# First blocks scored against their own 64 keys, and four steps of the opening list moved, in a fused attention and expert kernel

## The chip, the cores and the metric

The kernel runs on one core of a Trainium2 chip. The metric is the device time of one execution in microseconds (us); lower is better. Instruction names below are those of the profile: PE is TensorE (PEld its weight loads), DVE is VectorE, ACT is ScalarE, POOL is GpSimd and SP is SyncE.

## The reference

Two stages follow one another. The first is causal attention with a sliding window of 64 positions, for 8 batches, 8 heads, 576 positions and 64 values a head. The second takes the 4608 rows of 512 values through two weight matrices with a gate between them.

```python
scores = scale * np.matmul(q, k.transpose(0, 1, 3, 2))       # scale = 1/8
rel = pos[:, None] - pos[None, :]
mask = (rel >= 0) & (rel < 64)
scores = np.where(mask, scores, -1000000000.0)
attn = softmax(scores);  attn_out = attn @ v                 # (8, 8, 576, 64)
x = attn_out.transpose(0, 2, 1, 3).reshape(4608, 512)
h = x @ w_in                                                 # 512 -> 2048
out = (h * np.cos(h)) @ w_out                                # 2048 -> 512
```

## The kernel before, in words

**Attention.** The 576 positions of a head are cut into 9 blocks of 64. A *unit* (b, p, j) is block j of a pair p of heads in batch b: 128 rows (two heads) of queries. A block sees its own 64 keys and the 64 before them, so the scores of a unit are a tile of 128 rows and 128 columns. Block 0 has no keys before it; it is given the 128 keys from position 0, and the mask (line 323, `mask[:, 0]`, whose second half is the constant `NEG`) removes the second 64. There are 32 such first blocks, 4 in each batch.

Units are worked in groups of up to four (`groups`). A group n passes through these functions, whose names in the opening list stand in brackets: `g_scores` (s, Gs) lets PE write the scores into a PSUM bank; `g_max` (m, Gm) adds the mask on DVE and takes the row's extreme, into a tile `s`; `g_exp` (e, Ge) takes the exponential on ACT with its row sum `den`, into a tile `e` (6 buffers); `g_inv` (i, Gi) takes the reciprocal of the sums on DVE; `g_norm` (n, Gn) multiplies, on POOL or DVE, into a tile `w`; `g_trans` (w, Gw, Gc) transposes `w` on PE or by a DMA of SP; `values` (v, V) multiplies with v on PE. Groups 0 to 7 (`n < n_first`, batch 0) get their mask from an extra matmul into PSUM instead, and their exponentials read PSUM directly.

For b = 0 and 1 the two heads of a pair are scored by two matmuls of 64 rows each (L309), which run side by side in two halves of the array; transposes of q and k for these batches (tq, tk, Tq, Tk; L216) are of the same kind. From b = 2 on, one matmul with 128 rows does both heads (L303).

**The second stage** works in 9 tiles of 512 tokens. `first` and `first_half` (h; L448, L412) make h, ACT its sine (S; L590, L418), DVE the product (g; L593, L424), and `second_part` (o; L431) and L604 the output. Attention for the batch ahead is worked between the matmuls of a tile.

**Order.** Each engine runs its instructions in the order in which they are recorded. From tile 1 on, a plan with due times (`at`, `pump`) sets it. The start and tile 0 follow a list written out by hand, `FIRST` (lines 50 to 72), of steps such as `Tk.3` (transpose k of batch 1, pair 3), `Pk.3.d` (copy it out on DVE), `Gs.16.4` (scores of group 16 into bank 4), `o.1.0` (second quarter of output block 0: four matmuls), `Lwi.2` (third load of w_in, issued from POOL's queue), `n.1.0.p` (normalise the first group of pair 1 on POOL) and `yB.p` (copy a piece of batch 1's v to the other half of the partitions on POOL). Groups 9 to 16 are batch 1: 9, 11, 13, 15 hold blocks 0 to 3 of the four pairs, 10, 12, 14, 16 blocks 4 to 6; 8 is the last block of batch 0, and 17 and 18 are blocks 7 and 8 of batch 1.

Of the kernel before, what the change touches and what calls it, by code (L numbers as in the profile page):

```python
# [10 lines left out]
def _safe_warn(msg, *a, **kw):  # L11
# [5 lines left out]
AF = mybir.ActivationFunctionType  # L17
# [34 lines left out]
    "Lq0.2 tq.1 tk.1 m.0.0 pq.1.a ms.3.d s.0.1.1 Lk0.2 tq.2 pk.1.d s.1.0.2 Lq0.3 Lk0.3 tk.2 s.1.1.3 "  # L52
    "e.0.0 tq.3 m.0.1 Lq1.0 Lk1.0 Lq1.1 pq.2.d pk.2.d Lk1.1 tk.3 m.1.0 s.2.0.4 Lv0.0 Lv0.1 Tq.0 Lv0.2 "
    "pk.3.d m.2.0 e.0.1 pq.3.a i.0.0 e.1.0 Tk.0 s.3.0.0 Tq.1 e.2.0 Lv0.3 Lwi.0 Pq.0.d i.1.0 Lwi.1 m.3.0 "
    "m.1.1 i.2.0 Pk.0.a e.3.0 Lwi.2 Tk.1 n.1.0.p s.2.1.1 Pq.1.d Gs.10.2 m.2.1 Gs.9.4 n.0.0.p Pk.1.a "
    "n.2.0.p i.3.0 e.1.1 w.0.0 zA.0.d w.1.0 c.0.0.d Gs.12.0 w.2.0 n.3.0.p i.0.1 c.1.0.d zA.1.d c.2.0.d "
    "e.2.1 zB.0.s zB.1.s n.0.1.p i.1.1 w.3.0 v.0.0 c.3.0.d x.0.0.a s.3.1.3 Gm.10 v.1.0 m.3.1 i.2.1 "
    "Gs.11.2 Gm.9 Gm.12 n.1.1.p x.1.0.a e.3.1 ms.4.d w.0.1 w.1.1 c.1.1.a i.3.1 h.0.0.1 h.0.1.4 tb "
# [2 lines left out]
    "g.0.3 S.0.4 ms.6.d h.0.6.0 h.1.1.3 S.0.5 S.1.0 Lq1.2 S.0.6 g.0.4 S.1.1 g.1.0 h.1.2.2 Lk1.2 ms.7.d "  # L61
    "Lq1.3 h.0.7.4 g.0.5 h.1.3.1 Lv1.0 Lwo.1 g.1.1 S.1.2 h.1.4.3 g.0.6 Lk1.3 S.0.7 h.1.5.0 g.1.2 h.1.6.2 "
    "Lwo.2 g.0.7 S.1.3 S.1.4 S.1.5 Lwo.3 h.1.7.4 Lv1.1 S.1.6 g.1.3 g.1.4 S.1.7 g.1.5 Lv1.2 g.1.6 tb2 "
    "Tk.2 Lv1.3 Pk.2.d Ge.10 Tq.2 Pq.2.d Tq.3 Ge.9 Ge.12 o.0.0.1 Pq.3.d Tk.3 o.1.0 Pk.3.d Lv0.4 Lq2.0 "
    "Ge.11 Gs.14.3 Gi.10 Gm.14 g.1.7 Lq2.1 Gs.13.0 Lq2.2 o.0.1.2 Gi.9 o.2.0 Ge.14 Gn.10.p Gm.13 Gc.10 "
    "Gi.12 Gs.8.3 o.1.1 Gs.16.4 Gm.8 o.3.0 Ge.13 o.2.1 Gs.15.0 Gi.11 oc.0.d Gn.9.p o.3.1 Gn.12.p o.0.2.3 "
    "Gi.14 Gm.15 Gs.17.1 oc.1.d Gc.9 Gn.11.p Gi.13 Gm.16 o.1.2 Ge.8 Ge.16 Ge.15 y.1.d Gn.14.p yA.p Gi.8 "
    "Gc.12 Gm.17 o.0.3.0 Gi.16 Gn.13.p yB.p Gc.11 Gn.8.p Lq2.3 Lq2.4 Lq2.5 o.2.2 Gn.16.d Gw.8 Gc.14 "
    "Gc.13 Lk2.0 Gp.8.d o.3.2 Gi.15 Gw.16 Lk2.1 Ge.17 Lk2.2 o.1.3 Gn.15.d V.0 Gp.16.d oc.2.a Gw.15 Gi.17 "
    "Lk2.3 o.2.3 V.1 Gp.15.d X.0.a Gn.17.d X.1.d V.2 V.3 X.2.a X.3.d Gc.17 o.3.3 oc.3.a Gs.18.4 Gm.18 "  # L70
    "Ge.18 Lk2.4 Gi.18 Gn.18.d Gc.18 Lk2.5 Lv1.4 "
# [4 lines left out]
def kernel(  # L76
# [9 lines left out]
    nc = tc.nc  # L86
    B, H, S, D = q.shape
    assert (B, H, S, D) == (8, 8, 576, 64)
    scale = 1.0 / math.sqrt(D)
# [28 lines left out]
    mask = const.tile([128, 3, 128], F32, name="mask")  # L118
# [14 lines left out]
    def bank(which, name):  # L133
        return ps.tile([128, 512], F32, tag=which, name=name)
# [133 lines left out]
    groups = [[(0, p, j) for j in range(GF * g, GF * g + GF)] for p in range(PAIRS) for g in range(TU // GF)]  # L268
    n_first = len(groups)
# [12 lines left out]
    def g_scores(n, which):  # L282
        s_ps = bank((BANKS if n < n_listed else S_BANKS)[which], "s_ps")
        units = groups[n]
        if n == FILL[1]:
            nc.tensor.matmul(out=s_ps, lhsT=ident, rhs=mask16[:, 0:4].rearrange("p u c -> p (u c)"), start=True, stop=True,
                             skip_group_check=True)
        s_ps = s_ps[:, 0:len(units) * 128].rearrange("p (u c) -> p u c", c=128)
        if n < n_first:
            m0 = 2 if units[0][2] else 0  # L290
            for h in range(2):
                d = slice(64 * h, 64 * h + 64)
                nc.tensor.matmul(out=s_ps[d].rearrange("p u c -> p (u c)"), lhsT=ident[d, d],
                                 rhs=mask16[d, m0:m0 + len(units)].rearrange("p u c -> p (u c)"),
                                 start=True, stop=False, skip_group_check=True)
        for u, (b, p, j) in enumerate(units):
            kt = st["kT", b, p]
            lo = max(64 * j - 64, 0)
            rhs = kt[:, lo:lo + 128].rearrange("d (a t) -> d a t", a=2)
            if j and j % 2 == 0:  # L300
                rhs = rhs[:, ::-1, :]
            if b > 1:
                nc.tensor.matmul(out=s_ps[:, u].rearrange("p (a t) -> p a t", a=2),  # L303
                                 lhsT=qblocks[(b % 2) * PAIRS + p][:, j].rearrange("d h t -> d (h t)"), rhs=rhs,
                                 start=True, stop=True, skip_group_check=True)
                continue
            for h in range(2):
                d = slice(64 * h, 64 * h + 64)
                nc.tensor.matmul(out=s_ps[d, u].rearrange("p (a t) -> p a t", a=2),  # L309
                                 lhsT=qtiles[b * PAIRS + p][d, 64 * j:64 * j + 64], rhs=rhs[d], start=n >= n_first,  # L310
                                 stop=n >= n_first or u == len(units) - 1, skip_group_check=True)
        st["s", n] = s_ps


    def g_max(n):
        s_ps, units = st["s", n], groups[n]
        negm = att.tile([128, GF], F32, tag="negm", name="negm", bufs=8)
        if n < n_first:
            nc.vector.tensor_reduce(out=negm[:, 0:len(units)], in_=s_ps, op=ALU.max, axis=AX.X, negate=True)  # L319
        else:  # L320
            s = att.tile([128, GF, 128], F32, tag="s", name="s", bufs=4)
            for u, (b, p, j) in enumerate(units):
                nc.vector.tensor_tensor_reduce(out=s[:, u], in0=s_ps[:, u], in1=mask[:, 2 - j % 2 if j else 0],  # L323
                                               scale=-scale if b else -1.0, scalar=BIG, op0=ALU.add, op1=ALU.min,
                                               accum_out=negm[:, u:u + 1])
            st["s", n] = s
        st["m", n] = negm

    def g_exp(n):
        s, negm = st.pop(("s", n)), st.pop(("m", n))  # L330
        e = att.tile([128, GF, 128], F32, tag="e", name="e", bufs=6)
        den = att.tile([128, GF], F32, tag="den", name="den", bufs=8)
        for u in range(len(groups[n])):
            nc.scalar.activation(e[:, u], s[:, u], AF.Exp, bias=negm[:, u:u + 1], scale=1.0 if n < n_first else -1.0,  # L334
                                 accum_out=den[:, u:u + 1])
        st["e", n] = e, den

    def g_inv(n):
        e, den = st["e", n]
        rden = att.tile([128, GF], F32, tag="rden", name="rden", bufs=8)  # L340
        nc.vector.reciprocal(out=rden[:, 0:len(groups[n])], in_=den[:, 0:len(groups[n])])  # L341
        st["r", n] = rden
# [141 lines left out]
    n = n_listed  # L484
    for t in range(1, B - 1):
        last = max(i for i, units in enumerate(groups) if units[0][0] == t + 1)
        time = T * t + Q - 1.4
        for i in range(last + 1 - n):
            time += PACE * len(groups[n - 1]) if i else 0
            at(time, g_scores, n, i % 3)  # L490
            lags = LAGS[:2] + tuple(T * t + T - 0.79 - time + 0.01 * s for s in range(3)) if n == last else LAGS
            for lag, fn in zip(lags, (g_max, g_exp, g_inv)):
                at(time + lag, fn, n)
            at(time + lags[3], g_norm, n, "d" if n == n_listed + 5 else "p")
            at(time + (4.6 if n in direct else lags[-1]), g_trans, n)
            if n in direct:
                at(time + 4.9, g_put, n)
            ready.update({unit: time + (5.9 if n in direct else 8.5) for unit in groups[n]})
            n += 1
# [43 lines left out]
    def spread_first(lo, hi):  # L543
# [14 lines left out]
             "yA": lambda engine: spread_v(1, 0, engine, 0, 2), "yB": lambda engine: spread_v(1, 0, engine, 2, 3),  # L558
             "y": lambda half_, engine: spread_v(1, half_, engine),
             "s": lambda p, g, which: g_scores(2 * p + g, which), "m": lambda p, g: g_max(2 * p + g),  # L560
             "e": lambda p, g: g_exp(2 * p + g), "i": lambda p, g: g_inv(2 * p + g),
             "n": lambda p, g, engine: g_norm(2 * p + g, engine), "w": lambda p, g: g_trans(2 * p + g),
             "c": lambda p, g, engine: g_put(2 * p + g, engine), "v": values_half, "x": put_x_half,
             "tb": sine_table, "tb2": exp_table, "h": first_half, "S": sine_half, "g": gate_half,
             "Gs": g_scores, "Gm": g_max, "Ge": g_exp, "Gi": g_inv, "Gn": g_norm, "Gw": g_trans, "Gc": g_trans,
             "Gp": g_put, "V": lambda p: values(1, p), "X": lambda p, engine: put_x(1, p, engine),
             "o": second_part, "oc": put_out}
# [6 lines left out]
    for mt in range(1, n_mt):  # L574
# [5 lines left out]
        for ff in range(n_ff):  # L580
# [8 lines left out]
            e = ff % 2  # L589
# [5 lines left out]
        for ms0 in range(0, MT // 128, 2):  # L595
            o_sb = moe.tile([128, 2, d_model], F32, tag="out", name="out_sb", bufs=OUTS)
            o_ps = [bank(which, "out_ps") for which in (("O1",) if mt == n_mt - 1 and ms0 else ("O1", "O0"))]
            for e in range(2):
# [4 lines left out]
                for ff in range(n_ff):  # L603
                    nc.tensor.matmul(out=o_ps[e], lhsT=gT[ff // 2][:, ff % 2, ms * 128:ms * 128 + 128],  # L604
                                     rhs=w_out_sb[:, ff], start=ff == 0, stop=ff == n_ff - 1)
# [38 lines left out]
```

## Time and profile before

| what | value |
|---|---|
| median of 3 runs | 310.9 us (310.04 to 311.4) |
| profiled execution | 310.1 us, span of the instructions 308.3 us |
| granted TensorE clock | 1.0 |
| PE / DVE / ACT / POOL busy | 294.8 / 229.8 / 235.9 / 192.6 us |
| score matmuls of 128 rows (L303) | 216 recorded, 219 ns each |
| mask and extreme on DVE (L323) | 256, 286 ns each |
| exponentials (L334) | 256 and 32, 388 and 381 ns each |
| normalisation on POOL (L348) | 47 of 512 columns at 1041 ns, 27 of 384 at 826 ns |

Busy time is the union of an engine's instructions; a matmul's own duration holds its way through the array, so matmuls in a stream start closer together than they last. A row of a timeline gives the start, the time until its last instruction ends, and the number of instructions. Some matmul records can be missing.

### The profile page before, as it was taken

How to read it: one execution, taken by the hardware profiler on the slowest of the kernel's cores; microseconds unless marked ns; L12 is line 12 of the kernel's file. 1: busy time of each engine (PE TensorE's matmuls, PEld its weight loads, DVE VectorE, ACT ScalarE, POOL GpSimd, SP SyncE). 2: the span in 40 equal slices, each digit the busy share in tenths (PEclk: the TensorE clock that was granted, in tenths of full speed). 3: DMA queues.
4: the chain of work that ended last, by engine and by line, in shares of the span. 5: the costliest groups of instructions: out<-in, count | busy, mean ns of one | idle time of the engine just before them, and what ended most of it. 6: DMA issues, size and time to landing. Idle time of an engine off the chain costs nothing.

```text
span 308.3 us, 7893 instructions
## 1 busy us (share of the span) xinstructions
PE 294.8 (96%) x2584; PEld 159.5 (52%) x2616; DVE 229.8 (75%) x880; ACT 235.9 (77%) x785; POOL 192.6 (62%) x228
## 2 busy tenths in 40 slices
PE   3789999999999999999999999999999999999996
PEld 2668844545555555445544545455545554454443
DVE  5898988689778976798579867987698768335801
ACT  4998699677997799779976997699869986116600
POOL 8899569995559669967997799949902940000000
DMA  7999999999989997999999999999995534011011
GB/s 147 182 208 174 195 185 128 126 149 165 242 114 120 155 220 90 118 122 232 151 95 127 203 192 87 156 159 213 106 134 136 135 74 149 2 68 70 1 64 72
DMA packets 159945, 42.14 MB, mean 137 GB/s; under 512 B 148256, under 2 KB 155168, under 8 KB 159904
## 3 DMA queue, kind: packets, MB, share of 16 engines
q0 software_dynamic: 100192, 18.06, 83.4%
q1 hardware_dynamic: 59568, 23.38, 43.1%
q8 instruction: 20, 0.33, 0.5%
q14 instruction: 21, 0.17, 0.2%
q10 hardware_dynamic: 144, 0.20, 0.2%
HBM read 36.70 MB, written 9.44 MB: 150 GB/s over the span
## 4 chain that ended last, share of the span: by engine, by line
PE 89%; DVE 3%; ACT 2%; DMA 2%; issue 2%; POOL 1%; DVEq 0%; POOLq 0%; ACTq 0%
PE h_ps L448 35%; PE out_ps L604 34%; PE s_ps L303 4%; PE h_ps L412 4%; PE out_ps L431 3%; PE o_ps L379 3%; DMA k<-in_k_dram 2%; PE tq_ps L219 1%; PE out_ps L460 1%; PE s_ps L309 1%; ACT e L334 1%; PE tk_ps L216 1%; DVE negm L319 1%; DVE v L137 1%; DVE s L323 1%
## 5 line engine op out<-in xcount | busy, mean ns | idle before, releaser
L604 PE MATMUL out_ps<-w_out,gT 128*128 128x512 bf16 x482 | 115.0, 379 | 0.8 <-issue 0.2
L448 PE MATMUL h_ps<-xT,w_in 128*128 128x512 bf16 x498 | 114.5, 379 | 1.0
L334 ACT ACTIVATE e<-s,negm 128x128 f32<-128x128 f32 x256 | 98.6, 388 | 0.6 <-DVE negm L323 0.6
L590 ACT ACTIVATE sin<-h_ps 128x512 f32<-128x512 f32 x128 | 73.7, 598 | 32.2 <-PE h_ps L448 30.8
L593 DVE TENSOR_TENSOR gT<-h_ps,sin 128x512 bf16<-128x512 f32 x128 | 82.0, 684 | 21.8 <-ACT sin L590 21.1
L348 POOL TENSOR_TENSOR w<-e,rden 128x512 bf16<-128x512 f32 (+1 forms) x74 | 70.0, 962 | 34.8 <-DVE rden L341 33.7
L448 PEld LDWEIGHTS <-w_in 128*128 128x128 bf16 x512 | 48.8, 98 | 54.7 <-issue 0.4
L604 PEld LDWEIGHTS <-gT 128*128 128x128 bf16 x496 | 45.9, 98 | 44.2
L323 DVE CUSTOM_DVE_ANT_0 s<-s_ps,mask 128x128 f32<-128x128 f32 x256 | 58.4, 286 | 1.5 <-PE s_ps L309 1.0
L334 ACT ACTIVATION_READ_ACCUMULATOR e<-s,negm 128x1 f32 x256 | 48.1, 188 | 0.0
L182 POOL DMA_DIRECT2D q<-in_q_dram x36 | 28.3, 785 | 11.8 <-DMA q<-in_q_dram 4.4
L188 POOL DMA_DIRECT2D v<-in_v_dram x40 | 34.4, 878 | 0.5 <-DMA q<-in_q_dram 0.4
L182 POOL DMA_DIRECT2D k<-in_k_dram x36 | 28.1, 781 | 5.2 <-DMA k<-in_k_dram 4.5
L137 ACT COPY out_sb<-out_ps 128x512 f32<-128x512 f32 (+1 forms) x18 | 10.1, 564 | 24.5 <-PE out_ps L604 18.4
L341 DVE RECIPROCAL rden<-den 128x4 f32<-128x4 f32 (+1 forms) x79 | 13.7, 173 | 19.7 <-ACT e L334 15.4
L303 PEld LDWEIGHTS <-qB 128*128 128x128 bf16 x216 | 17.1, 98 | 14.2
L137 DVE CAST xT<-o_ps 128x512 bf16<-128x512 f32 x24 | 15.5, 676 | 9.4 <-PE o_ps L379 9.3
L137 DVE COPY out_sb<-out_ps 128x512 f32<-128x512 f32 x18 | 12.4, 689 | 12.9 <-PE out_ps L604 12.5
L303 PE MATMUL s_ps<-kT,qB 128*128 128x128 bf16 x216 | 21.9, 219 | 0.0
L323 DVE DVE_READ_ACCUMULATOR2_ANT negm<- 128x1 f32 x256 | 21.2, 83 | 0.0
L137 POOL COPY v<-v 64x1536 bf16<-64x1536 bf16 (+3 forms) x12 | 18.8, 1570 | 0.3
L137 DVE COPY qB<-tq_ps 64x384 bf16<-64x384 bf16 (+1 forms) x40 | 15.6, 390 | 0.4
(69 smaller groups left out, 252.1 us busy)
## 6 DMA issues: line engine op xcount, KB each, us to landing
out_dram<-out_sb SPq DMA_DIRECT2D x16, 512.0 KB, 7.8
v<-in_v_dram POOLq DMA_DIRECT2D x32, 128.0 KB, 6.1
q<-in_q_dram POOLq DMA_DIRECT2D x36, 96.0 KB, 8.6
k<-in_k_dram POOLq DMA_DIRECT2D x36, 96.0 KB, 9.0
w_in<-in_moe_w_in_dram POOLq DMA_DIRECT2D x4, 512.0 KB, 9.5
w_out<-in_moe_w_out_dram POOLq DMA_DIRECT2D x4, 512.0 KB, 10.9
wT<-w SPq DMA_TRANSPOSE x68, 4.7
q<-in_q_dram POOLq DMA_DIRECT2D x7, 144.0 KB, 6.4
```

Source lines behind the costliest of these rows:

```text
L137: {"a": nc.scalar.copy, "p": nc.gpsimd.tensor_copy}.get(engine, nc.vector.tensor_copy)(out, in_)
L182: nc.gpsimd.dma_start(out=st[name, b][:, c].rearrange("p (h d) -> p h d", h=H), in_=src.rearrange("h p d -> p h d"))
L188: nc.gpsimd.dma_start(out=vt.rearrange("p (h d) -> p h d", h=H), in_=v[b, :, c * 128:c * 128 + n, :].rearrange("h p d -> p h d"))
L303: nc.tensor.matmul(out=s_ps[:, u].rearrange("p (a t) -> p a t", a=2), lhsT=qblocks[(b % 2) * PAIRS + p][:, j].rearrange("d h t -> d (h t)" ...
L323: nc.vector.tensor_tensor_reduce(out=s[:, u], in0=s_ps[:, u], in1=mask[:, 2 - j % 2 if j else 0], scale=-scale if b else -1.0, scalar=BIG, ...
L334: nc.scalar.activation(e[:, u], s[:, u], AF.Exp, bias=negm[:, u:u + 1], scale=1.0 if n < n_first else -1.0, accum_out=den[:, u:u + 1])
L341: nc.vector.reciprocal(out=rden[:, 0:len(groups[n])], in_=den[:, 0:len(groups[n])])
L348: (nc.gpsimd if engine == "p" else nc.vector).tensor_tensor(out=w[:, 0:u], in0=e[:, 0:u], op=ALU.mult, in1=rden[:, 0:u].unsqueeze(2).to_br ...
L448: nc.tensor.matmul(out=st["h", ff], lhsT=w_in_sb[:, ks, ff * 128:ff * 128 + 128], rhs=st["xT", mt][:, ks], start=start, stop=stop)
L590: nc.scalar.activation(sin, h_ps, AF.Sin, bias=math.pi / 2.0)
L593: nc.vector.tensor_tensor(out=gt[:, e], in0=h_ps, in1=sin, op=ALU.mult)
L604: nc.tensor.matmul(out=o_ps[e], lhsT=gT[ff // 2][:, ff % 2, ms * 128:ms * 128 + 128], rhs=w_out_sb[:, ff], start=ff == 0, stop=ff == n_ff - 1)
```

## The change

The first part concerns the functions. For a unit with j = 0, `g_scores` multiplies with its own 64 keys only and writes 64 columns. For groups whose mask is added on DVE, `g_max` and `g_exp` work on those 64 columns, and `g_inv` sets the other 64 columns of `e` to zero on DVE ahead of the reciprocal, so that `g_norm` and what follows stay as they are. Batch 0's first blocks lie in groups with `n < n_first`: their exponentials keep 128 columns, whose second half holds the mask alone.

The second part moves steps in `FIRST`. `Lwi.2` goes behind `Tk.1` and `n.1.0.p`; on POOL, the load is now issued after the first normalisation. `Tk.3` goes behind `o.1.0`, where it stands on PE directly ahead of `Gs.14`. `Gs.16.4` and `o.1.1` change places, so that `Gs.16` stands on PE directly behind `Gs.8`. `yB.p` goes behind `Gn.8.p`, which is therefore the earlier of the two on POOL.

```diff
-    "m.1.1 i.2.0 Pk.0.a e.3.0 Lwi.2 Tk.1 n.1.0.p s.2.1.1 Pq.1.d Gs.10.2 m.2.1 Gs.9.4 n.0.0.p Pk.1.a "
+    "m.1.1 i.2.0 Pk.0.a e.3.0 Tk.1 n.1.0.p Lwi.2 s.2.1.1 Pq.1.d Gs.10.2 m.2.1 Gs.9.4 n.0.0.p Pk.1.a "
...
-    "Tk.2 Lv1.3 Pk.2.d Ge.10 Tq.2 Pq.2.d Tq.3 Ge.9 Ge.12 o.0.0.1 Pq.3.d Tk.3 o.1.0 Pk.3.d Lv0.4 Lq2.0 "
+    "Tk.2 Lv1.3 Pk.2.d Ge.10 Tq.2 Pq.2.d Tq.3 Ge.9 Ge.12 o.0.0.1 Pq.3.d o.1.0 Tk.3 Pk.3.d Lv0.4 Lq2.0 "
     "Ge.11 Gs.14.3 Gi.10 Gm.14 g.1.7 Lq2.1 Gs.13.0 Lq2.2 o.0.1.2 Gi.9 o.2.0 Ge.14 Gn.10.p Gm.13 Gc.10 "
-    "Gi.12 Gs.8.3 o.1.1 Gs.16.4 Gm.8 o.3.0 Ge.13 o.2.1 Gs.15.0 Gi.11 oc.0.d Gn.9.p o.3.1 Gn.12.p o.0.2.3 "
+    "Gi.12 Gs.8.3 Gs.16.4 o.1.1 Gm.8 o.3.0 Ge.13 o.2.1 Gs.15.0 Gi.11 oc.0.d Gn.9.p o.3.1 Gn.12.p o.0.2.3 "
...
-    "Gc.12 Gm.17 o.0.3.0 Gi.16 Gn.13.p yB.p Gc.11 Gn.8.p Lq2.3 Lq2.4 Lq2.5 o.2.2 Gn.16.d Gw.8 Gc.14 "
+    "Gc.12 Gm.17 o.0.3.0 Gi.16 Gn.13.p Gc.11 Gn.8.p yB.p Lq2.3 Lq2.4 Lq2.5 o.2.2 Gn.16.d Gw.8 Gc.14 "
...
@@ g_scores
-            lo = max(64 * j - 64, 0)
-            rhs = kt[:, lo:lo + 128].rearrange("d (a t) -> d a t", a=2)
+            lo, chunks = max(64 * j - 64, 0), 2 if j else 1
+            rhs = kt[:, lo:lo + 64 * chunks].rearrange("d (a t) -> d a t", a=chunks)
...
-                nc.tensor.matmul(out=s_ps[:, u].rearrange("p (a t) -> p a t", a=2),
+                nc.tensor.matmul(out=s_ps[:, u, 0:64 * chunks].rearrange("p (a t) -> p a t", a=chunks),
...
-                nc.tensor.matmul(out=s_ps[d, u].rearrange("p (a t) -> p a t", a=2),
+                nc.tensor.matmul(out=s_ps[d, u, 0:64 * chunks].rearrange("p (a t) -> p a t", a=chunks),
@@ g_max
-                nc.vector.tensor_tensor_reduce(out=s[:, u], in0=s_ps[:, u], in1=mask[:, 2 - j % 2 if j else 0],
+                c = slice(0, 128 if j else 64)
+                nc.vector.tensor_tensor_reduce(out=s[:, u, c], in0=s_ps[:, u, c], in1=mask[:, 2 - j % 2 if j else 0, c],
@@ g_exp
-        for u in range(len(groups[n])):
-            nc.scalar.activation(e[:, u], s[:, u], AF.Exp, bias=negm[:, u:u + 1], scale=1.0 if n < n_first else -1.0,
+        for u, (_, _, j) in enumerate(groups[n]):
+            c = slice(0, 128 if j or n < n_first else 64)
+            nc.scalar.activation(e[:, u, c], s[:, u, c], AF.Exp, bias=negm[:, u:u + 1], scale=1.0 if n < n_first else -1.0,
@@ g_inv
+        for u, (_, _, j) in enumerate(groups[n]):
+            if j == 0 and n >= n_first:
+                nc.vector.memset(e[:, u, 64:128], 0.0)
```

## The prediction

> **What bounds the kernel now.** I read the page first: busy shares and the chain that ended last.
>
> ```profile
> PE 294.8 (96%) x2584; PEld 159.5 (52%) x2616; DVE 229.8 (75%) x880; ACT 235.9 (77%) x785; POOL 192.6 (62%) x228
> ...
> PE 89%; DVE 3%; ACT 2%; DMA 2%; issue 2%; POOL 1%; DVEq 0%; POOLq 0%; ACTq 0%
> ```
>
> PE is busy 96% of a span of 308.3 us and carries 89% of the chain. Then the chain in order of time, to see whether PE's own rate or a wait sets each piece:
>
> ```profile
> 65.26 0.26 PE tq_ps L219 x6
> ...
> 76.85 0.22 PE s_ps L303 x4
> ```
>
> Both are streams: 6 matmuls with 96 moving columns in 0.26 us (0.042 each), 4 with 128 columns in 0.22 (0.056 each). Between 62 and 302 us almost nothing but PE stands in the chain, so a shorter PE instruction there shortens the run. Next PE's timeline in tile 0, where the moved jobs lie:
>
> ```profile
> 45.28 1.90 PE L431 MATMUL out_ps<-w_out,gT 128*128 128x512 bf16 x8
> 47.11 0.41 PE L309 MATMUL s_ps<-kT,qT 64*64 64x128 bf16 x8
> 47.45 1.90 PE L431 MATMUL out_ps<-w_out,gT 128*128 128x512 bf16 x8
> ...
> 52.56 0.40 PE L359 MATMUL tw_ps<-ident,w 128*128 128x128 bf16 x4 [0.17 <-POOL w L348]
> 52.79 1.03 PE L431 MATMUL out_ps<-w_out,gT 128*128 128x512 bf16 x4
> 53.65 0.33 PE L359 MATMUL tw_ps<-ident,w 128*128 128x128 bf16 x3
> ```
>
> The reader compares starts. From 52.79 to 53.65 four 512-column matmuls take 0.86, so 0.216 each; a full-array job (L359) beside them costs nothing extra. From 45.28 to 47.11 eight take 1.83, 0.10 above 8 x 0.216: entering a 64-row job (L309) costs 0.10. That job takes 0.34 to the next L431, where its four pairs, 0.052 apart in the trace, are worth 0.21: 0.13 more to begin and leave. The same start differences stand at every 64-row job. Last, POOL's timeline before the wait at 52.56:
>
> ```profile
> 49.45 1.04 POOL L348 TENSOR_TENSOR w<-e,rden 128x512 bf16<-128x512 f32 x1
> 50.43 1.07 POOL L137 COPY v<-v 64x512 bf16<-64x512 bf16 x1
> 51.47 1.03 POOL L348 TENSOR_TENSOR w<-e,rden 128x512 bf16<-128x512 f32 x1
> ```
>
> The copy of a piece of v stands ahead of the normalisation (Gn.8) whose end PE awaits.
>
> **The change, part by part.**
>
> *First blocks, scores on PE.* b=2 to 7 have 4 pairs each: 24 matmuls of L303 go from 128 to 64 moving columns. The saving per matmul is bounded below by 0.056-0.042 = 0.014 (the 96-column stream shows that a 128-column weight load fits in 0.042) and above by half of 0.053, 0.027. Streams of 64 columns elsewhere (tk_ps L216, o_ps L379) start a pair every 0.029, so I take 0.026: 24 x 0.026 = 0.62 us, bounds 0.33 to 0.65, all on the path. For b=0 and 1 the pairs shrink from 0.052 to 0.029; only Gs.13 and Gs.15 lie where PE is the limit: 2 x 0.023 = 0.05. The other six lie before 25 us, where PE waits for others: nothing.
>
> *Vector and scalar work.* I read the groups with shapes kept apart:
>
> ```profile
> L323 DVE CUSTOM_DVE_ANT_0 s<-s_ps,mask 128x128 f32<-128x128 f32 x256 | 58.4, 286 | 1.5 <-PE s_ps L309 1.0
> ...
> L303 PE MATMUL s_ps<-kT,qB 128*128 128x128 bf16 x216 | 21.9, 219 | 0.0
> ...
> L151 DVE MEMSET mask<- 128x64 f32 x1 | 0.1, 112 | 0.0
> ```
>
> For b=1 to 7, 28 of L323 lose 64 columns. The PSUM copies of 512 and 128 columns took 689 and 290 ns, 1.04 a column, so 0.067 each, 1.9 us of DVE. 28 memsets of 128x64 come in, 112 ns each by L151's row: 3.1 us. Net +1.2 us at most over seven tiles, beside 25.6 busy of 32 us in a tile. 28 exps on ACT lose 64 columns; ACT's copies of 512 and 384 columns took 569 and 479, 0.7 a column, so 0.045 each, 0.18 a tile, off the path. The memset stands ahead of the reciprocal and waits for POOL's normalisation six groups back; queued behind it are that reciprocal and the next scores, and POOL waits for the reciprocal. But the exp of the same group waits for the same buffer, and the reciprocal waits for that exp (15.4 us over 27 waits, 0.57 each): the memset runs in that wait. On the path: 0, and 0.08 each in tile 0 where DVE runs without a gap; without the cover it would be 28 x 0.11 = 3.1 us of DVE.
>
> *Two 64-row jobs joined.* Tk.3 now stands against Gs.14, Gs.16 against Gs.8. Each loses an entry (0.094), a slower first pair (0.022), an exit (0.096) and 0.010 on the next matmul: 0.22, together 0.44. Tk.3 runs 0.86 later, so its copy on DVE starts at 41.32, not 40.55; behind it wait a reciprocal, Gm.14, g.1.7 (DVE 42.38, now about 42.77 to 43.44) and Gm.13. DVE catches up by 45.7, where a reciprocal waited for ACT anyway. Gs.16 moves forward to about 43.66 and needs the bank that g.1.7 frees: 0.2 to spare.
>
> *The piece of v (yB).* PE reaches Gw.8 at 52.23 and starts at 52.56: 0.33 idle. Gn.8 started at 51.47, after the copy; its reciprocal was done at 51.25. With PE 0.49 earlier, DVE's part moves 0.44 (its out_ps copy at 48.52 waits for PE), the reciprocal is done near 50.8, Gn.8 ends near 52.0 and PE starts near 52.0: 0.55 in place of 0.49, with 0.3 of idle left. The order alone is worth 0.06 to 0.3. yB then ends near 52.5; values at 54.2 need it. Of yB's later end the loads Lq2.3 onwards feel nothing worth counting (start 52.45); the last q piece landed at 57.75, and PE wants it at 60.6.
>
> *The third w_in load (Lwi.2).* POOL idled until 14.32, when its queue slot came free, and issued at 14.60; the first w came at 15.41 though its reciprocal was done at 14.32. Now w runs first and Lwi.2 goes out near 15.4. The load lands behind the two issued at 12.34 and 13.09 (landed 20.65, 23.86, then 26.81), so 0.8 later in the queue costs nothing; PE needs it at 27.5. If it did not hide: at most 0.1 to 0.2. What PE waits for there, the copied v rows, landed at 25.41 (PE 25.50), and that copy is not touched. Gain 0, up to 0.05.
>
> Sum: 0.55 + 0.62 = 1.17, less rounding 1.15. The profiled execution took 310.1 (span 308.3, 1.8 around it); it would be 308.95. The median of the three runs is 310.9, 0.8 above; from there 309.7. About 0.5% (1.55 us) is what a measurement of this kernel can tell from no change, so this is a gain just inside it.
>
> **The rivals.**
>
> *Weight loads set the pace.* If the next weights need 0.056, shorter streams save nothing on L303: gain 0.55, 310.3. For it: L303's load row (98 ns) is longer than a stream. Against: L219 loads 128 columns every 0.042. [...] Chance 0.08.
>
> *Key transposes hold PE.* The third kT piece of b=2 landed at 73.44, read at 73.82; that of b=4 landed at 137.46 and PE waited 0.04. If landings do not move with PE, all won before 137 is lost, and 16 matmuls x 0.026 = 0.4 remain: 310.5. Against: SP issues them behind wT of Gs.18, which follows PE. Chance 0.08.
>
> *Faster than the sum.* DVE's v copy in the start waited for POOL:
>
> ```profile
> 17.79 0.81 DVE L137 COPY v<-v 64x512 bf16<-64x512 bf16 x1
> ...
> 19.35 0.29 DVE L137 COPY v<-v 64x512 bf16<-64x512 bf16 x1
> ```
>
> The first is 0.5 longer than its twin and ends just after POOL's w does (18.45). Earlier w's could free 0.25 on the chain there, and the 0.3 left at Gw.8 could go too: 1.7, 309.2. Against: ACT is busy to 21.88 and starts the next chain piece at 21.94. Chance 0.17.
>
> *Slower: the memsets queue behind POOL.* If a memset waits like that copy until POOL's 1.04 us instruction ends, it costs 0.5 on average. In tile 0 three stand ahead of Gn.8's reciprocal: 1.5. In each of six later tiles four delay DVE by 2 us, against wT slacks of 0.4 (154.16) and 0.6 (90.47): I price 0.3 a tile, 1.8. Total -1.15+1.5+1.8 = +2.2: 313.1. It decides once memsets average over 0.4 us. For it: the v copy. Against: no memset of the trace ran beside a POOL w, and the eight of 576 all took 538. [...] Chance 0.15.
>
> **How the numbers follow.** The sum 0.52, weight loads 0.08, key transposes 0.08, faster 0.17, slower 0.15. Runs spread by 0.7 either way, so 0.08 of the sum's chance falls past the 0.5% line. Faster 0.17+0.08 = 0.25; same 0.44+0.08+0.08 = 0.60; slower 0.15. Range 308.3 (1.7 and 0.9 of scatter) to 312.0 (310.5, scatter, part of the slower case); the sum alone: 309.0 to 310.5.
>
> **What would show it.** Memset rows near 112 ns; L303 with 64 columns starting the next matmul 0.029 on (0.042 or 0.056: the bounds); in tile 0 an L216 x18 followed at once by L309 x14, and Gs.8 with Gs.16 as one L309 x14; Gw.8 near 52.0; tile 1's first scores 0.55 earlier than 73.65. Wrong if the memsets run to half a us, if PE idles before L303 on kT, or if Gs.16 waits for g.1.7.

## The result, and the profile after

The changed kernel took 313.67 us, median of 6 runs (311.34 to 314.48), beside 309.81 for the kernel before on the same chip (6 runs, 308.93 to 311.4): a ratio of 1.0112, 95% interval 1.0079 to 1.0146. By that ratio it is 3.5 us slower, where 1.15 less was forecast; the time lies above the range. The profiled execution took 313.2, its span 311.4 (308.3 before). Two runs far above all others, 406.71 of the kernel before and 318.01 of after_noport, stand outside the ratios below.

The page first, the same two rows as before:

```profile
PE 298.5 (96%) x2616; PEld 160.7 (52%) x2616; DVE 230.7 (74%) x908; ACT 234.6 (75%) x785; POOL 192.3 (62%) x228
...
PE 82%; DVE 7%; ACT 6%; DMA 3%; issue 1%; POOL 0%; SPq 0%; DVEq 0%; POOLq 0%; ACTq 0%
```

PE lost 7 points of the chain to DVE, ACT and DMA, although the change only takes work off PE. The boundaries of the stages say where, read from PE's timeline in both kernels:

| stretch | before, us | after, us | difference |
|---|---|---|---|
| start, to the first long stream of h (L412, now L417) | 27.45 | 29.45 | +2.00 |
| from there to tile 1's first h | 31.08 | 30.78 | -0.30 |
| tile 1 | 32.26 | 34.21 | +1.95 |
| tiles 2 to 6 together | 157.94 | 157.41 | -0.53 |

Gains stand where they were forecast (0.30 of 0.55 in tile 0, and 0.53 in tiles 2 to 6, where all of tiles 1 to 6 were to bring 0.62). Two losses of 2 us stand against them, at places where the prediction had put nothing.

**The start.** DVE's timeline, where zA.0 and zA.1 (the two `v<-v` copies) stand with the copies of `wT` that follow:

```profile
17.29 2.10 DVE L137 COPY v<-v 64x512 bf16<-64x512 bf16 x1
19.32 0.41 DVE L137 COPY wT<-tw_ps 128x512 bf16<-128x512 bf16 x1
...
20.15 0.93 DVE L137 COPY v<-v 64x512 bf16<-64x512 bf16 x1
```

They took 0.81 and 0.29 before. POOL's timeline in the same stretch, the kernel before in the first row:

```profile
15.41 6.12 POOL L348 TENSOR_TENSOR w<-e,rden 128x512 bf16<-128x512 f32 x6
...
14.39 1.04 POOL L353 TENSOR_TENSOR w<-e,rden 128x512 bf16<-128x512 f32 x1
15.38 0.80 POOL L204 DMA_DIRECT2D w_in<-in_moe_w_in_dram  x1
16.20 3.03 POOL L353 TENSOR_TENSOR w<-e,rden 128x512 bf16<-128x512 f32 x3
19.89 1.04 POOL L353 TENSOR_TENSOR w<-e,rden 128x512 bf16<-128x512 f32 x1 [0.65 <-DVE rden L346]
```

Before, six normalisations stood back to back behind Lwi.2, and the copy still got in at the first boundary between two of them. Lwi.2 now follows one normalisation, and three stand back to back behind it, until 19.23. The first copy asked 0.09 into the second of these, let the third go ahead of it as well, and ended 0.16 after that. By then POOL had stopped: its next normalisation waits for a reciprocal that stands behind the copy on DVE (the 0.65 in the row of 19.89). The second copy ended 0.15 after the normalisation that ends at 20.93. PE's timeline shows what that holds up:

```profile
17.31 0.62 PE L364 MATMUL tw_ps<-ident,w 128*128 128x128 bf16 x8 [0.95 <-POOL w L353]
...
19.77 0.38 PE L362 MATMUL tw_ps<-ident 128*128 128x128 bf16 x4 [1.02 <-DVE wT L137]
...
21.13 0.38 PE L403 MATMUL o_ps<-wT,v 128*64 128x64 bf16 x12 [0.57 <-DVE v L137]
...
23.52 1.04 PE L364 MATMUL tw_ps<-ident,w 128*128 128x128 bf16 x8
```

PE idles behind both copies, and then the eight transposes that took 0.62 at 17.31 take 1.04 at 23.52. From 23.52 to 24.56 the granted clock was 0.50. The table by stretches shows it too (PE's busy time stands third, the granted clock third from the end). The kernel before, then the changed one:

```profile
17.00:22.00 5.00, 4.23 (x84) 3.15 (x85) 4.91 (x20) 4.85 (x23) 4.54 (x5) 1.00 1.25 207
22.00:26.00 4.00, 3.61 (x52) 3.06 (x50) 3.45 (x26) 3.97 (x13) 3.67 (x5) 1.00 1.10 205
...
17.00:22.00 5.00, 3.11 (x49) 2.12 (x51) 4.71 (x10) 3.94 (x20) 3.45 (x5) 0.94 1.25 207
22.00:26.00 4.00, 4.00 (x56) 3.35 (x53) 3.93 (x31) 3.01 (x12) 3.16 (x4) 0.65 0.84 176
```

PE was busy 4.23 of the first 5 us before and 3.11 after.

**Tile 1.** PE's timeline at the values of batch 2, which ran without a gap before (first row):

```profile
89.57 1.20 PE L379 MATMUL o_ps<-wT,v 128*64 128x64 bf16 x64
...
91.48 0.38 PE L384 MATMUL o_ps<-wT,v 128*64 128x64 bf16 x12
92.10 0.99 PE L384 MATMUL o_ps<-wT,v 128*64 128x64 bf16 x36 [0.24 <-DMA wT<-w]
93.69 0.32 PE L384 MATMUL o_ps<-wT,v 128*64 128x64 bf16 x8 [0.60 <-DMA wT<-w]
94.19 0.32 PE L384 MATMUL o_ps<-wT,v 128*64 128x64 bf16 x8 [0.18 <-DMA wT<-w]
```

From the first of them to tile 2's first h PE took 2.96 us, 1.23 before. The transposes of `w` that SP issues land late, beside the q and k loads for batch 3. The last of these landed at 91.49, 31.3 us after tile 1's first h; before it was 84.96, 26.4 after it. POOL issues them behind the loads for batch 2, and its timeline in tile 0 shows why the whole row starts later:

```profile
51.19 1.03 POOL L353 TENSOR_TENSOR w<-e,rden 128x512 bf16<-128x512 f32 x1
53.16 1.04 POOL L353 TENSOR_TENSOR w<-e,rden 128x512 bf16<-128x512 f32 x1 [0.93 <-DVE rden L346]
54.14 0.94 POOL L137 COPY v<-v 64x512 bf16<-64x512 bf16 x1
55.02 2.33 POOL L182 DMA_DIRECT2D q<-in_q_dram  x3
```

The second row is Gn.8. Before, yB filled the time in which Gn.8 waits for its reciprocal; now POOL idles 0.93 there and yB comes after. Lq2.3, one of the loads for batch 2, goes out 5.21 us ahead of tile 1's first h, where it was 6.08.

### The profile page after: what moved, and what is told of

It is laid out like the page before. It is cut to its first block, busy times and chain, and to the rows that moved or that the text cites. A ratio compares the mean times of both kernels' runs of the same rounds, so it can differ in the third digit from the quotient of the medians.

```text
span 311.4 us, 7904 instructions
## 1 busy us (share of the span) xinstructions
PE 298.5 (96%) x2616; PEld 160.7 (52%) x2616; DVE 230.7 (74%) x908; ACT 234.6 (75%) x785; POOL 192.3 (62%) x228
## 4 chain that ended last, share of the span: by engine, by line
PE 82%; DVE 7%; ACT 6%; DMA 3%; issue 1%; POOL 0%; SPq 0%; DVEq 0%; POOLq 0%; ACTq 0%
PE h_ps L453 31%; PE out_ps L609 30%; ACT e L336 5%; PE h_ps L417 5%; PE out_ps L436 4%; DVE gT L598 3%; PE s_ps L303 3%; PE o_ps L384 3%; DMA wT<-w 2%; DVE v L137 1%; PE s_ps L309 1%; PE out_ps L465 1%; DVE qB L137 1%; DMA rows<-in_k_dram 1%; PE tq_ps L219 1%; PE tk_ps L216 1%
## 5 line engine op out<-in xcount | busy, mean ns | idle before, releaser
L609 PE MATMUL out_ps<-w_out,gT 128*128 128x512 bf16 x496 | 117.3, 379 | 0.0
L336 ACT ACTIVATE e<-s,negm 128x128 f32<-128x128 f32 (+1 forms) x256 | 97.1, 381 | 0.6 <-DVE negm L324 0.6
L324 DVE CUSTOM_DVE_ANT_0 s<-s_ps,mask 128x128 f32<-128x128 f32 (+1 forms) x256 | 56.3, 278 | 1.4 <-PE s_ps L309 0.7
L303 PE MATMUL s_ps<-kT,qB 128*128 128x128 bf16 (+1 forms) x216 | 21.4, 216 | 0.2 <-DMA kT<-k 0.2
```

The source lines that it names most:

```text
L303: nc.tensor.matmul(out=s_ps[:, u, 0:64 * chunks].rearrange("p (a t) -> p a t", a=chunks), lhsT=qblocks[(b % 2) * PAIRS + p][:, j].rearrang ...
L324: nc.vector.tensor_tensor_reduce(out=s[:, u, c], in0=s_ps[:, u, c], in1=mask[:, 2 - j % 2 if j else 0, c], scale=-scale if b else -1.0, sc ...
L336: nc.scalar.activation(e[:, u, c], s[:, u, c], AF.Exp, bias=negm[:, u:u + 1], scale=1.0 if n < n_first else -1.0, accum_out=den[:, u:u + 1])
```

## The experiments

The theory: Lwi.2's move makes DVE's copies of v wait longer for POOL's normalisations (called "port" in the expectations, which is a name: why such a copy waits, no run shows), PE's idle time and the drop of its clock follow, and yB's move adds the late loads. Rivals: the 64-key work shifts the start; all of it is late loads; the lateness of the w_in load itself; chance. PE's clock is given as the number of runs whose mean granted clock was under 0.998; the five profiles with one drop, 3.41 us at 0.50, have a mean of 0.994 or 0.995.

This table holds what the traces show for each kernel with a profile: the lengths of zA.0 and zA.1, the begin of the long h stream, and the length of tile 1 (where two names stand, the kernel was profiled twice).

| kernel | zA.0, zA.1 | stream | tile 1 | clock drops |
|---|---|---|---|---|
| before | 0.81, 0.29 | 27.45 | 32.26 | 7 of 128 |
| changed, after_again | 2.10, 0.93; 2.11, 0.93 | 29.45; 29.92 | 34.21; 34.08 | 8 of 12 |
| only_lwi | 2.11, 0.93 | 29.66 | 32.26 | 4 of 6 |
| after_no_yb, after_no_yb_2 | 2.23, 0.93; 2.15, 0.93 | 28.15; 29.39 | 32.15; 32.15 | 8 of 16 |
| lwi_n2 | 0.26, 2.00 | 28.91 | 32.26 | 4 of 10 |
| lwi_delay | 0.22, 0.29 | 26.88 | 32.26 | 5 of 10 |
| lwi_noport | 0.65, 0.68 | 26.96 | 32.26 | 0 of 12 |
| after_noport | 0.65, 0.68 | 27.98 | 33.92 | 1 of 11 |
| only_func, func_kt | 0.49, 0.29; 0.47, 0.29 | 26.36; 27.31 | 32.15; 32.49 | 1 of 13 |
| only_joins | 0.29, 0.31 | 26.60 | 32.26 | 1 of 12 |
| only_yb | 0.74, 0.29 | 28.15 | 32.50 | 0 of 12 |
| after_no_lwi | 0.95, 0.29 | 26.73 | 33.25 | 0 of 10 |
| func_joins | 0.60, 0.29 | 27.27 | 33.38 | 1 of 12 |
| no_lwi_lq3 | 0.86, 0.29 | 27.08 | 32.46 | 1 of 12 |
| func_kt_early | 0.52, 0.29 | 26.16 | 32.16 | 0 of 12 |
| lq3_kt_early | 0.30, 0.85 | 26.90 | 32.16 | 0 of 12 |

**Each part alone.** only_lwi, only_func, only_joins and only_yb are the kernel before with one part of the change:

```diff
# only_lwi
-Lwi.2 Tk.1 n.1.0.p s.2.1.1
+Tk.1 n.1.0.p Lwi.2 s.2.1.1
# only_func: g_scores, g_max, g_exp, g_inv as in the change, FIRST as before
# only_joins
-Tk.3 o.1.0 ... Gs.8.3 o.1.1 Gs.16.4
+o.1.0 Tk.3 ... Gs.8.3 Gs.16.4 o.1.1
# only_yb
-yB.p Gc.11 Gn.8.p
+Gc.11 Gn.8.p yB.p
```

> The kernel before with one edit: Lwi.2 behind Tk.1 and n.1.0.p. Theory (port): this step alone makes POOL's normalisations run back to back under DVE's first copy of a piece of v (zA.0), which then waits through two of them: zA.0 near 2.1 us in place of 0.8, the x96 stream of L412 begins near 29.5 in place of 27.45, and part of the second loss (tile 1) follows from the later start; time +2 to +4 us, 311.8 to 313.8. Rival (functions): the 64-key work shifts the start, and this step is worth 0: zA.0 near 0.8, 309.8. Rival (loads): only the late issue of Lq2.3 behind yB costs, 309.8 here too.

> The kernel before with the 64-key functions alone, FIRST as before. Theory (port): zA.0 stays near 0.8, the steady gain of about 0.1 us a tile stands, no new wait for wT or kT: 309.1 (0.7 less than 309.8). Rival (functions): the 64-column scores shift DVE against POOL in the start, zA.0 near 2.1 and the x96 stream 2 us late: 311.5 to 313.7. Rival (loads): 309.1.

> The kernel before with Tk.3 behind o.1.0 and Gs.16 behind Gs.8. All theories: nothing of the start changes, so zA.0 and the stream's begin as before (27.45 within 0.3); the joins save up to 0.44 us in tile 0, and the wait at Gw.8 or the later piece may give some of it back: 309.4 to 309.8. If it comes out over 310.5, the joins delay something behind them that no theory names.

> The kernel before with yB behind Gn.8 only. Theory (port): start as before; Lq2.3 goes out about 0.1 us later at most, since POOL does the same two steps in the other order: 309.5 to 309.8. Rival (loads): the order of POOL delays Lq2.3 by a us or more, and the loads behind it run into tile 1's wT transposes: waits of PE at L379 near 90 us, and +1.5 to +2 us, 311.3 to 311.8.

Measured against the kernel before: only_lwi 1.0087 (1.0060 to 1.0114), so +2.7 us; only_func 0.9983 (0.9961 to 1.0006); only_joins 1.0017 (1.0000 to 1.0034); only_yb 1.0013 (0.9987 to 1.0038). The moved load is most of the loss by itself, the functions and joins are not part of it, and the memsets cost nothing. In only_lwi tile 1 took 32.26 as before, so the late start brings nothing of the second loss, against its expectation. Of yB's move this comparison only says that it isn't worth 2 us alone; in only_yb Lq2.3 went out 0.88 later against tile 1's first h, where at most 0.1 was expected.

**One part taken back.** after_no_lwi and after_no_yb are the changed kernel with Lwi.2, or yB, where it was:

```diff
# after_no_lwi
-Tk.1 n.1.0.p Lwi.2 s.2.1.1
+Lwi.2 Tk.1 n.1.0.p s.2.1.1
# after_no_yb, after_no_yb_2
-Gc.11 Gn.8.p yB.p
+yB.p Gc.11 Gn.8.p
```

> The changed kernel with Lwi.2 back ahead of Tk.1. Theory (port): the first copy of v (zA.0) takes under 0.9 us again, PE's clock stays at 1.0 between 22 and 26 us, the x96 stream begins near 26.5 to 27.5, and the time is that of the other parts together, 309.0 to 310.0. Rival (the parts interact, and the wT and kT landings of tile 1 are late for their own reason): PE still waits about 2 us in tile 1, 311.0 to 311.8.

> The changed kernel with yB back ahead of Gn.8. Theory (port): zA.0 stays near 2.1 us and the time above 312.0. Rival (loads): with Lq2.3 out about 0.9 us earlier against PE, the loads keep clear of tile 1's wT transposes, the 2.0 us of waits in tile 1 go, and the time is 311.3 to 312.0; zA.0 as in the changed kernel.

after_no_lwi came to 1.0013 (0.9989 to 1.0037), 310.39 where at most 310.0 was expected: without Lwi.2's move almost all of the loss is gone, and the copies and the clock are as before, although tile 1 still takes 1.1 us more than the 32.15 of the functions. after_no_yb came to 1.0031 (1.0000 to 1.0062), better than either theory had it: tile 1 was back at 32.15, but only 2 of its 10 runs had a clock drop. So it was run again beside the changed kernel on one chip:

> The changed kernel once more, for a second profile and more runs. Theory (port, then PE's clock): zA.0 near 2 us again, half or more of the runs with a mean clock under 0.998, median 312.3 to 313.7. If the first profile's 2.0 us of wT waits in tile 1 belongs to the change and not to that run, they stand here too; if to the run, tile 1's restart comes 32.2 to 33.4 us after tile 0's end.

> The changed kernel with yB back ahead of Gn.8, once more beside the changed kernel on one chip. Theory (yB costs through the late loads): at least 1.0 us faster than the changed kernel, 311.0 to 312.0. Rival (yB is worth nothing that can be measured and the first comparison met more clock drops on one side): within 0.5 us of it at the same share of clock drops.

after_again: 1.0110 (1.0080 to 1.0140), median 312.81. after_no_yb_2: 1.0062 (1.0040 to 1.0085), median 311.46, with a clock drop in all 6 of its runs against 4 of 6. yB's move therefore costs 1.4 us here (medians of 6 and 6), and it isn't the clock that makes it. In tile 1 the five profiles with yB moved and Lq2.3 behind it took 0.24, 1.1, 1.8, 1.9 and 2.1 us more than the undisturbed tile; of twelve profiles with yB in its old place ten took nothing more, one 0.3 and one (func_joins) 1.2. Late loads are the rule in the one and the exception in the other. The last of batch 3's q and k loads goes with it in all nineteen profiles. Where it landed 26.1 to 28.3 us after tile 1's first h (twelve profiles), the values took 1.23 to tile 2's first h; at 28.3 and 28.7 (no_lwi_lq3 and only_yb) 1.5; at 29.0 to 31.3 (the other five, func_joins among them) 2.2 to 3.0. That these loads slow the transposes is argued from this order, not shown by a run of its own.

**The wait for POOL, by itself.** lwi_delay and lwi_n2 shift the instant or the place; lwi_noport takes the wait away:

```diff
# lwi_delay: only_lwi, and
-w.0.0 zA.0.d
+w.0.0 dl zA.0.d          # dl: nc.vector.memset(junk, 0.0), junk 128x288 f32
# lwi_n2: the kernel before, and
-Lwi.2 Tk.1 n.1.0.p ... n.2.0.p i.3.0
+Tk.1 n.1.0.p ... n.2.0.p Lwi.2 i.3.0
# lwi_noport: only_lwi, and in spread_v for zA
-            copy(engine, to, of)
+            nc.vector.tensor_reduce(out=to, in_=of.rearrange("p a (d o) -> p a d o", o=1), axis=AX.X, op=ALU.max)
# after_noport: the changed kernel with the same edit
```

> The kernel before with Lwi.2 moved as in the change, and one more DVE instruction directly ahead of zA.0: a memset of 128x288 (estimated 0.3 us from the rows 112 ns for 64 and 538 ns for 576 columns) into a tile that nothing reads. It only shifts the instant at which the copy asks. Theory (port, decided by the instant): the copy starts 0.3 to 0.4 us into a POOL normalisation as in the kernel before and waits for that one alone: zA.0 0.8 us, clock 1.0 between 22 and 26, 309.4 to 310.4. Rival (back-to-back normalisations always win): zA.0 about 1.8 us and ending at the same time, 312.0 to 312.8.

> The kernel before with Lwi.2 moved further, behind n.2.0.p, so that on POOL a load stands between the normalisation under which zA.0 begins and the next. Theory (port): the copy waits for one normalisation at most, zA.0 0.3 to 0.8 us, 308.9 to 309.8. Rival (the later load itself costs: w_in lands late): PE waits on w_in between 26 and 30 us, 311 or more.

> The kernel before with Lwi.2 moved as in the change, and the two DVE copies zA.0 and zA.1 written as a maximum over an axis of length one (the same values): in place of 0.29 us undisturbed, an estimated 0.6 each (the 512-column reductions L319 took 0.68 from PSUM). Theory (port: the copy form waits for POOL's normalisations): the reductions take their 0.6 whatever POOL does, the x96 stream begins near 27 to 28, the clock stays 1.0, and the time falls from the 312.2 of the moved load to 309.7 to 310.5. Rival (the moved load itself, or the instant of its landing, delays the start): still 311.5 to 312.5. Rival (any DVE work on SBUF waits for POOL): the reductions take about 2 us and the time is 312 or more.

> The whole change, with the two copies zA written as a maximum over an axis of length one. Theory (port): the start is mended (copies 0.65, x96 stream near 26.5 to 27.2, clock 1.0), and what is left is the other three parts as in the changed kernel with Lwi.2 back (310.4): 309.5 to 310.6. Rival (late loads cost most of the loss): still 311.5 or more.

lwi_noport settles it. DVE's timeline, with the reductions in place of the copies, under the same row of POOL normalisations (five back to back from 16.26 to 21.40):

```profile
17.53 0.65 DVE L201 TENSOR_REDUCE v<-v 64x512 bf16<-64x512 bf16 x1
...
18.94 0.68 DVE L201 TENSOR_REDUCE v<-v 64x512 bf16<-64x512 bf16 x1
```

and its table by stretches:

```profile
17.00:22.00 5.00, 4.09 (x84) 3.13 (x85) 4.91 (x19) 4.63 (x22) 4.35 (x6) 1.00 1.23 212
22.00:26.00 4.00, 4.00 (x57) 3.47 (x55) 3.60 (x27) 3.97 (x13) 3.68 (x5) 1.00 1.11 204
```

The load is as late as in only_lwi, the reductions took 0.65 and 0.68 beside POOL's row (the first ended while a normalisation was still running), the clock stays up in all 12 runs, and the ratio is 1.0011 (0.9991 to 1.0031) in place of 1.0087. The late landing of w_in is thereby ruled out, and so is the idea that any DVE work on SBUF waits. after_noport, expected at 309.5 to 310.6, came to 311.06, 1.0042 (1.0020 to 1.0065): the copies are mended, the stream begins at 27.98 in the profile (26.5 to 27.2 expected), and tile 1 is 33.92 us long. That execution (313.08) was the slowest of the eleven that the ratio counts, so its tile 1 may be longer than usual.

lwi_n2 missed its expectation: zA.0 got through in 0.26, but zA.1 then waited for two normalisations behind the load (2.00), and the ratio is 1.0052 (1.0027 to 1.0077). lwi_delay was half a miss: its profile shows 0.22 for zA.0, no wait at all where the theory had one normalisation and 0.8, but that execution (310.37) was the fastest of ten; the median is 311.69, 1.0060 (1.0037 to 1.0084), with a clock drop in half of the runs. One profile doesn't stand for its kernel where the outcome differs from run to run.

**What holds the functions' gain.** func_joins drops both POOL moves; no_lwi_lq3 puts Lq2.3 into POOL's idle 0.93; func_kt is only_func once more; the last two bring the kT transposes of batches 3 to 6 forward.

```diff
# no_lwi_lq3: after_no_lwi, and
-Gn.8.p yB.p Lq2.3 Lq2.4
+Lq2.3 Gn.8.p yB.p Lq2.4
# func_kt_early: only_func, and lq3_kt_early: no_lwi_lq3, and
-c - 5.5), turn_k, b, c)
+c - (6.3 if b > 2 else 5.5)), turn_k, b, c)
```

> The changed kernel without its two POOL moves: the 64-key functions and the two joins, Lwi.2 and yB as before. Theory: zA.0 under 0.95 us; Lq2.3 6.1 us ahead of tile 1's restart as in the kernel before, so no wait for wT in tile 1; tiles 1 to 6 each 0.1 us shorter, with one wait for kT of about 0.6 in tile 3 as in the run of the functions alone; the joins alone brought nothing: 308.7 to 309.4. If the joins hurt by themselves: 309.5 to 310.

> The changed kernel with Lwi.2 back, and with Lq2.3 issued ahead of Gn.8 on POOL, in the 0.93 us that POOL idles since yB moved. Theory (late loads: the burst of q and k loads of batch 2 starts 0.88 us later against PE since yB moved, and runs into the wT transposes of tile 1): with the first of them 2 us earlier, PE's waits in tile 1 fall from 1.0 us to under 0.4, and the time from 310.3 to 309.2 to 309.8. Rival (the waits of tile 1 have nothing to do with the burst): 1 us of waits stays, 310.0 to 310.7.

> The kernel before with the 64-key functions alone, a second look. Theory: the gain of 0.1 us a tile stands, and PE's wait for kT of batch 4 at the first scores of tile 3 (0.6 to 0.7 us in the first look) stands again, so that the functions bring 0.5 us or less in all: 308.3 to 309.3.

> The 64-key functions alone, with the kT transposes of batches 3 to 6 due 0.8 steps earlier in the plan. Theory (the kT wait of tile 3 takes the functions' gain): tile 3 comes to 31.55 us in place of 32.27, and the time to 308.0 to 308.8, faster than the kernel before by 0.3 to 0.5%. Rival (the queue is the limit: earlier transposes only delay the wT ahead of or behind them): waits for wT in its place, 308.8 to 309.6.

> Functions, joins and yB's move with Lwi.2 as before, Lq2.3 ahead of Gn.8 and the kT transposes 0.8 steps earlier. Theory: tile 0 0.25 shorter, tile 1 without long waits, tile 3 31.55: 307.9 to 308.8, the best of all. Rival (as above): 309.0 to 309.6 as without the earlier kT.

func_joins: 1.0003 (0.9981 to 1.0025), a miss, with a tile 1 that is 1.2 us longer, most of it at values that wait for wT, which no theory gave it. no_lwi_lq3: 0.9986 (0.9963 to 1.0008), tile 1 at 32.46, as the late loads would have it. func_kt took 309.73, one run, and missed too: its tile 3 took 31.67, so the wait for kT did not stand again, and its tile 1 took 0.34 more. In only_func, PE's timeline at the start of tile 3:

```profile
136.00 0.30 PE L303 MATMUL s_ps<-kT,qB 128*128 128x64 bf16 x3
136.88 0.22 PE L303 MATMUL s_ps<-kT,qB 128*128 128x128 bf16 x1 [0.57 <-DMA kT<-k]
```

and in func_kt_early the same scores:

```profile
135.81 0.36 PE L303 MATMUL s_ps<-kT,qB 128*128 128x64 bf16 x4
136.01 1.89 PE L609 MATMUL out_ps<-w_out,gT 128*128 128x512 bf16 x8
```

The 0.57 is about as large as all that the functions gain. With the transposes earlier it is gone: func_kt_early runs at 0.9972 (0.9953 to 0.9990; 308.87, just above the 308.8 expected) and lq3_kt_early at 0.9976 (0.9953 to 0.9999). Both beat the kernel before by about 0.8 us, and the changed kernel by more than 4. Either keeps Lwi.2 where it was. That the earlier transposes make the gain is read from the traces; between only_func and func_kt_early the times alone (0.9983 and 0.9972) don't tell.

## Why the prediction was wrong, point by point

**The third w_in load: the step that failed.** "Gain 0, up to 0.05" priced the landing of the load, and that part was right: issued 0.78 later, it landed at 26.48 where it was 26.81, and lwi_noport has the same late issue without the loss. The term left out what the move does to DVE: the first copy of v, which waited only for the normalisation that was running, now waits until POOL runs out of normalisations, 2.10 in place of 0.81. The row of normalisations is not what is new, since six stood back to back before. The prediction saw the 0.81 of the copy in the trace and read it with the wrong sign: "Earlier w's could free 0.25 on the chain there", in the rival "faster". The move costs 2.7 us alone. Some 2.2 of it is the start in the profiles: streams begin at 28.15 to 29.92 where a copy let a second normalisation go ahead (six profiles, 29.25 on average), and at 26.16 to 28.15 elsewhere (27.06). The drop of PE's clock is a part of that and not always there: in only_lwi the four runs with it have a median of 312.5, the two without 311.1.

**The rival that came nearest by number was wrong.** "The memsets queue behind POOL", 313.1, named the wait for POOL but the wrong instruction. The row of the memsets:

```profile
L344 DVE MEMSET e<- x28: 112/112/112, 45.4 to 243.0; 128x64 f32 x28
```

All 28 took 112 ns, ten of them wholly while a normalisation ran, so a memset didn't wait for POOL here. Copies of v did: every delayed one ended 0.14 to 0.16 after a normalisation did, and in six profiles a copy which asked first let a later normalisation go ahead as well. The reductions that stood in their place in lwi_noport took 0.65 and 0.68. What sets such a copy apart from a memset and a reduction isn't shown.

**yB: a second step that failed.** "Of yB's later end the loads Lq2.3 onwards feel nothing worth counting" took the two POOL steps as the same work in another order. The prediction's own numbers said otherwise: the normalisation ahead of yB ended at 50.49, the reciprocal for Gn.8 was done at 51.25, and yB filled that gap. Moved, it leaves 0.93 idle, and the loads are 0.87 later against PE. The price is 1.4 us in the changed kernel; with Lwi.2 at its old place it can't be told from noise (after_no_lwi 1.0013, func_joins 1.0003). The gain at Gw.8 was about 0.05, between the tile 0 of func_joins (30.83) and of the changed kernel (30.78).

**Scores on PE: right.** 24 matmuls of 64 columns start the next one 28 or 29 ns on, where 128 columns take 56: the 0.62 is there, 0.10 a tile from tile 1 on. The rival "weight loads set the pace" is out.

**The rival "key transposes hold PE" was underrated at 0.08.** Of the ten profiles with the functions and the kT transposes at their old due time, seven have a tile 3 that is 0.5 to 1.4 us longer than the 31.55 without the wait, about as much as the whole steady gain or more; in the other three, the changed kernel's first profile among them, it is 0.1 at most.

**Joins: half the size.** The forecast was 0.44, of 0.55 in tile 0. Alone they gave nothing (31.14 against 31.08 before), with the functions 0.25. Joined jobs do appear in PE's timeline of the changed kernel:

```profile
42.84 0.47 PE L216 MATMUL tk_ps<-ident,k 64*64 64x64 bf16 x18
43.15 0.53 PE L309 MATMUL s_ps<-kT,qT 64*64 64x128 bf16 x14
...
45.44 0.58 PE L309 MATMUL s_ps<-kT,qT 64*64 64x128 bf16 x14
```

The rest went into the wait that the prediction left at 0.3: PE reaches Gw.8 earlier and waits there longer (0.40 marked in func_joins, 0.17 before).

**What stays open.** Why a copy gets in at the first boundary between two normalisations in ten profiles, but lets further ones go ahead in six, all with Lwi.2 moved, isn't settled. Two readings are left. One is the load: in the six it stands one or two normalisations ahead of the boundary on POOL, elsewhere three or four, but in lq3_kt_early the first copy got in behind two. The other is the instant: the copies that lost asked between 0.04 us before and 0.21 after the start of a normalisation, those that got in 0.23 to 0.94 after it. No run holds one fixed and moves the other. In lwi_delay the first copy asked 0.13 after a start and didn't wait; that normalisation took 1.25 in place of 1.04. This copy fits neither reading.

## What to carry to other kernels

Before an instruction of POOL is moved, look at what runs on DVE at the same time, and in which form (here the first copy of v took 2.10 us beside the row, and a reduction in its place 0.65): a row of a copy that is longer than its twin's (0.81 against 0.29) can point at a wait for the other engine, and a move on that engine can turn a wait for one instruction into a wait for several of them (0.81 became 2.10). yB filled an engine's idle time and was not free to move, even past one neighbour (1.4 us in the changed kernel); ask what is issued behind such a step. And a saving on the bound engine was kept here only as far as the transfers that feed it moved with it (the wait of 0.57 for kT was about as large as all that the functions gain).

## What the hardware showed

In the changed kernel's profile PE's granted clock fell to half for 3.41 us; PE's longest idle time in the 5 us ahead was 1.02. The stretch:

```profile
21.38:24.79 3.41, 3.41 (x54) 2.58 (x48) 3.34 (x25) 2.26 (x9) 2.38 (x3) 0.50 1.09 223
```

All five profiles with a drop show 0.50 for 3.41 us. In them PE was busy 2.7 to 3.5 of the 5 us from 17 to 22, and 1.82 to 1.90 of the 3.41 us directly ahead of the drop. These runs do not show what sets it off: the drop came in 29 of 54 runs with Lwi.2 moved and plain copies and in 4 of 95 of the variants with Lwi.2 in place, one profile (after_no_yb) had PE busy 3.35 of the 5 us and a clock of 1.00, and only_yb had PE busy 1.72 of the 3.41 us from 23.78 and no drop behind it.
